# Attention and two FFNs on one core: key sums moved to TensorE, products regrouped over the array's tiles, and new urgencies for the planner

## The chip, the core and the metric

One core of a Trainium2 chip runs the whole program. The metric is device microseconds (us) of one execution; the time of the kernel before is the median of three runs. Beside them one execution was profiled, and all rows below are of that one.

## The reference, cut to what matters

```python
q_lm = q.reshape(B, H, m, S // m, D).mean(axis=3)       # B=4, H=8, S=576, D=64, m=32
k_lm = k.reshape(B, H, m, S // m, D).mean(axis=3)       # sums over 18 neighbours
A, Bm, C = sm(q, k_lm), sm(q_lm, k_lm), sm(q_lm, k)     # sm = softmax(scale * a @ b.T)
Z = Bm.T / (norm_1(Bm) * norm_inf(Bm) + 1e-06)
for _ in range(6):
    Z = 2 * Z - Z @ Bm @ Z                              # inverse of Bm by Newton steps
x = A @ Z @ C @ v                                       # (2304, 512) after the heads are joined
h = x @ w_in;  x = maximum(0.01 * h, h) @ w_out         # first FFN, width 2048
# RMS norm, then silu(x @ w_gate) * (x @ w_val) @ w_out2, width 1536
```

## The kernel before

Nothing loops at run time. A planner in the kernel's own Python code (`Order`) writes out one instruction list for each engine. Each piece of work is a generator that yields its engine, a cost in ns and what it needs (`yield [("pe", 400)], [...]`), and then issues its instructions. Among the pieces that could start soon the planner takes the one with the least due time plus penalties; `PAR` holds the due times and, for each stretch of planned time, a window and a bias for VectorE (DVE), ScalarE (ACT) and GpSimd (POOL). For many pieces two or three engines may be named, and the planner chooses. `"pe"` is a full 128x128 product, `"pet"` a product on a part of the array ("tiled"); `TURN` is what the planner charges for a change between them. The costs decide the order only. On the chip every engine runs its list in that order and waits on semaphores.

The work of the batches of attention is called a chain. That of the first batch (`chain(0)`) stands alone at the start, before there is any other work for TensorE, and so sets when the first FFN can begin:

- `key_sums` and `sums` add 18 neighbouring columns of K and Q. For the first batch, K's are done by a halving add on POOL and a reduction on DVE.
- The scores Q_lm K^T (L653, four groups, each four products at 64x32 tiles) go to DVE for sums and to ACT for copies; then come softmax, norms, the Gram matrix (`gram`, L758), transposes of the exponentials (`turn`, L797), five Newton steps (L925, each followed by an add on DVE) and the sixth, folded into z (L895). C V is L825, its small transposes L864.
- `soft_a` (L976) makes the scores of A, `soft_rest` its softmax on DVE, POOL and ACT. It needs the key sums. For the first batch `times_z` (L1041) multiplies the result by z, and `split_a` writes it as a high and a low part, `at`.
- `form_first` (L1121) multiplies W_in by the small matrix of C V in four column pieces. The result is `mm`, which is split likewise.
- `ffn1_h` (L1168, six products of 128x288) multiplies `mm` and `at`; `ffn1_y` (L1239, twelve products) multiplies by W_out. These two fill TensorE until the gated FFN (L1641) and the output product (L1916). The chains of the batches 1 to 3 are strewn among them.
- Weights arrive in halves of 64-bit words and are turned into float32 by ACT (L496, L504), POOL and DVE (`convert`).
- `warm` issues spare products on a tile of ones (L1072), whose results nobody reads, wherever the planner sees TensorE free before the first FFN.

Each group of four heads takes four tiles of the array: `heads` gives for head h the rows of its operand and a strip `32 * (h ^ g)` of 32 partitions, so that in L1041 row strip and column strip of a product are the same, for both groups.

## Time and profile before

| | us |
|---|---|
| median of three runs | 792.68 (792.26 to 792.8) |
| the profiled execution | 791.7 |
| its span, first to last instruction | 789.6 |
| TensorE busy with products in that span | 777.4 |

The span is what the views count in; the execution's own time holds 2.1 us more around it. In the views PE is TensorE's products, PEld its weight loads. A float32 product leaves two records in the trace (a transpose, and a product of the type float32r, one), so counts there are twice those of the instruction list.

### The profile page before, as it was taken

To read this page: it belongs to the slowest core of one execution; us is meant where nothing else is said; L and a number is where in the kernel's file an instruction comes from. 1 tells how busy PE (TensorE), PEld (TensorE's weight loads), DVE (VectorE), ACT (ScalarE), POOL (GpSimd) and SP (SyncE) were. 2 spreads that over 40 slices of the span, in tenths; PEclk is the share of its full clock that TensorE was granted. 3 is DMA by queue.
4 is the path that set the end of the run, shared out by engine and by line. 5 is a ranking of instruction groups with operands and counts; after the bars stand their busy time and mean duration, and the time that the engine had idled before them with its cause. 6 is when DMAs were issued, how large, how long until landed. Compare 5 with 4: busy or idle time off the path is not lost.

```text
span 789.6 us, 16701 instructions
## 1 busy us (share of the span) xinstructions
PE 777.4 (98%) x6489; PEld 740.6 (94%) x6489; DVE 537.7 (68%) x1044; ACT 391.3 (50%) x862; POOL 219.8 (28%) x262
## 2 busy tenths in 40 slices
PE   5999999999999999999999999999999999999998
PEld 3788998899799998999999999999999999999998
DVE  6899966866631488876588666544357599997771
ACT  4887465555554565656643333234432265454440
POOL 2421000154575200035443533466541010000000
PEclk9999999999999999999999999999999999999999
DMA  9984645484653353544211433222331695535501
GB/s 327 364 288 145 240 137 168 117 285 155 181 171 131 108 194 127 191 126 129 81 41 64 164 114 114 94 68 86 114 115 41 193 330 174 169 115 167 154 28 54
DMA packets 84319, 119.71 MB, mean 152 GB/s; under 512 B 7824, under 2 KB 62608, under 8 KB 84240
## 3 DMA queue, kind: packets, MB, share of 16 engines
q1 hardware_dynamic: 84240, 118.64, 45.7%
q8 instruction: 51, 0.84, 0.4%
q14 instruction: 28, 0.23, 0.1%
HBM read 81.86 MB, written 36.77 MB: 150 GB/s over the span
## 4 chain that ended last, share of the span: by engine, by line
PE 96%; DVE 1%; DMA 1%; ACT 1%; issue 0%; SPq 0%
PE py L1239 25%; PE py L1641 19%; PE b L1641 14%; PE b L1168 13%; PE py L1916 10%; PE b L1916 7%; PE b L1096 2%; DMA kt<-kT 1%; PE b L925 1%; PE b L976 1%; PE b L1072 1%; PE b L797 1%; PE b L825 1%; PE b L653 1%; PE py L653 0%; PE b L1471 0%
## 5 line engine op out<-in xcount | busy, mean ns | idle before, releaser
L1239 PE MATMUL py<-gs,w 128*128 128x288 f32 x1536 | 222.9, 296 | 0.4 <-DVE w L89 0.4
L1239 PEld LDWEIGHTS py<-gs,w 128*128 128x128 f32 x1536 | 209.3, 188 | 5.5 <-issue 3.7
L1168 PE MATMUL b<-at,mm 128*128 128x288 f32 x768 | 119.9, 298 | 0.0
L1168 PEld LDWEIGHTS b<-at,mm 128*128 128x128 f32 x768 | 106.6, 188 | 7.9 <-issue 3.0
L1186 ACT ACTIVATE gs<-b 128x288 fp32r<-128x288 f32 x128 | 52.8, 412 | 105.0 <-PE b L1168 83.3
L89 POOL TENSOR_TENSOR gs<-hs,gs 128x288 fp32r<-128x288 f32 x60 | 53.0, 888 | 115.6 <-ACT hs L1189 86.5
L89 DVE TENSOR_TENSOR ct<-gs,py 128x384 f32<-128x384 f32 x72 | 39.6, 551 | 44.2 <-PE py L1641 42.6
L89 DVE TENSOR_TENSOR gs<-gs,py 128x384 f32<-128x384 f32 x72 | 39.7, 552 | 19.0 <-PE py L1641 17.9
L1189 ACT ACTIVATE hs<-b 128x288 f32<-128x288 f32 x128 | 52.5, 410 | 0.0
L1711 ACT ACTIVATE hs<-b 128x384 f32<-128x384 f32 x36 | 17.7, 491 | 68.8 <-PE b L1641 68.7
L89 POOL TENSOR_TENSOR misc<-misc 128x256 f32<-128x256 f32 (+2 forms) x44 | 34.5, 794 | 31.9 <-DVE misc L89 22.6
L89 DVE TENSOR_TENSOR gs<-hs,b 128x384 f32<-128x384 f32 (+1 forms) x45 | 23.6, 524 | 28.7 <-PE b L1641 24.3
L89 DVE TENSOR_TENSOR gs<-hs,gs 128x288 fp32r<-128x288 f32 x68 | 31.5, 463 | 16.3 <-ACT hs L1189 15.9
L89 POOL TENSOR_TENSOR mm<-misc,mm 128x512 fp32r<-128x512 f32 (+1 forms) x15 | 16.7, 1111 | 85.8 <-ACT mm L450 78.1
L450 ACT COPY hs<-b 128x384 f32<-128x384 f32 (+1 forms) x44 | 19.9, 452 | 36.8 <-PE b L1641 21.5
L1740 ACT ACTIVATE ct<-ct 128x384 f32<-128x384 f32 x36 | 18.9, 526 | 37.5 <-DVE ct L89 37.3
L1641 PE MATMUL b<-w,wt 128*128 128x384 f32 x180 | 35.4, 337 | 0.0
L1641 PE MATMUL b<-w,mm 128*128 128x384 f32 x180 | 35.4, 337 | 0.0
L496 ACT ACTIVATE raw<-raw 128x512 f32<-128x512 f32 x52 | 34.8, 678 | 0.4 <-DMA raw<-w_gate 0.4
L1641 PE MATMUL py<-w,wt 128*128 128x384 f32 x180 | 34.5, 338 | 0.0
L1641 PE MATMUL py<-w,mm 128*128 128x384 f32 x180 | 34.3, 336 | 0.0
L1641 PEld LDWEIGHTS b<-w,wt 128*128 128x128 f32 x180 | 31.9, 188 | 0.0
(306 smaller groups left out, 1594.2 us busy)
## 6 DMA issues: line engine op xcount, KB each, us to landing
u_dram<-us SPq DMA_DIRECT2D x36, 384.0 KB, 2.3
raw<-w_out SPq DMA_DIRECT2D x20, 512.0 KB, 4.4
y_dram<-ys SPq DMA_DIRECT2D x56, 144.0 KB, 2.1
yin<-u_dram SPq DMA_DIRECT2D x20, 384.0 KB, 5.2
raw<-w_gate SPq DMA_DIRECT2D x12, 512.0 KB, 4.0
raw<-w_val SPq DMA_DIRECT2D x12, 512.0 KB, 4.8
wo_dram<-raw SPq DMA_DIRECT2D x42, 128.0 KB, 2.0
qt<-qT SPq DMA_DIRECT2D x8, 576.0 KB, 4.9
```

The source lines that it names most:

```text
L89: self.last = make(*args, **kwargs)
L450: nc.scalar.copy(out, src)
L496: nc.scalar.activation(high.bitcast(F32), high.bitcast(F32), AF.Prelu, scale=2.0 ** -112, alpha=2.0 ** 32)
L1096: nc.tensor.matmul(pm[g][lm, :], wt_in[b, g][rows, p], w_in_sb[c][rows, 2 * g + p, :].bitcast(F32), start=True, stop=True,)
L1168: nc.tensor.matmul(ph[:, :SB], w[b, c][:, g, o:o + P], x[j][:, g, :], start=(n == 0), stop=(n == 3 * NG - 1),)
L1186: nc.scalar.activation(g_hi[u], ph[:, :SB], AF.Prelu, alpha=0.01)
L1189: nc.scalar.activation(hs, ph[:, :SB], AF.Prelu, alpha=0.01)
L1239: nc.tensor.matmul(yacc[i][d][:, :SB], w[f][:, d * P:(d + 1) * P], x[u], start=(f == f0 and n == 0), stop=(f == f1 - 1 and n == 2),)
L1641: nc.tensor.matmul(pp[:, :GB], w[f][:, i, c * P:(c + 1) * P], x[b][k][:, c, :], start=(first and n == 0), stop=(n == 5), skip_group_check= ...
L1711: nc.scalar.activation(sg, pp["a"][:, :GB], AF.Silu)
L1740: nc.scalar.activation(t["c12"], t["c12"], AF.Silu)
L1916: nc.tensor.matmul(pp[name][:, :HM], x[:, p, :], o_home[r][:, i, p, :], start=(tag is not None and m == 0), stop=(m == 3 * NP2 - 1), skip_ ...
```

## The change

Seven edits, all in code of the first batch but for the tables:

1. `key_sums`: instead of an add on POOL and a reduction on DVE, 18 products with the identity for each of the two groups add up the 18 neighbours in PSUM (128x128 weights, 64 columns, float32), in slices of six; ACT or DVE copies the result.
2. `soft_a` of the first batch writes head h to strip 32 h in both groups, `z` is made in the same layout (in two banks, copied out by two copies), and `times_z` multiplies row strip 32 h into column strip `32 * (h ^ g)`: the two groups lie on eight different tiles and no longer on the same four.
3. `warm` may issue a small tiled spare product where the last product was tiled.
4. Pieces of the first batch that were planned as full products are named tiled, with smaller costs: scores, Gram matrix, Newton steps, z, `times_z`, `form_first`.
5. `TURN` between two tiled pieces falls from 80 to 40.
6. All numbers in `PAR` are new.
7. `split_a` and the output step have slightly different planned costs.

```diff
-        [13.0, 1837, 1.2, 2906, -16456, 25637],
+        [13.0, 1517, 19.7, -11610, -23885, -30083],
...
-    TURN = {("pe", "pet"): 89, ("pet", "pet"): 80, ("pet", "pe"): 104}
+    TURN = {("pe", "pet"): 89, ("pet", "pet"): 40, ("pet", "pe"): 104}
...
-            half = et[:, g, :S].rearrange("p (a m t) -> p a m t", a=2, t=GRP // 2)
-            yield pool(S), [f"k0,{g}"]
             x = k_in[0, g][:, :, :S].rearrange("p a (m t) -> p a m t", t=GRP)
-            nc.gpsimd.tensor_add(half, x[..., :GRP // 2], x[..., GRP // 2:])
-            yield dve(S), []
-            nc.vector.reduce_sum(k_in[0, g][:, :, S:], half, axis=AX.X)
+            step = 6
+            for i in range(0, GRP, step):
+                yield [("pe", 112 * step)], [] if i else [("px", 1), f"k0,{g}"]
+                if i == 0:
+                    pk = bank("px")
+                for t in range(i, i + step):
+                    nc.tensor.matmul(
+                        pk[:, :2 * M], ident, x[..., t], start=(t == 0), stop=(t == GRP - 1)
+                    )
+            on = yield act(2 * M) + dve(2 * M), []
+            copy(on, k_in[0, g][:, :, S:], pk[:, :2 * M].rearrange("p (a m) -> p a m", m=M))
+            order.free(pk)
...
-                yield [("pe", 420)], [(pa, 1)]
-                pr = bank(pa)
+                yield [("pet", 330)], [(pa, NG)]
+                pz = [bank(pa) for _ in range(NG)]
...
-                                pr[lm, g * M:(g + 1) * M], rz[lm, 2, g, :], r,
+                                pz[g][M * h:M * h + M, :M], rz[lm, 2, g, :], r,
...
-            for _, p, rows, lm in heads(g):
+            for h4, p, rows, lm in heads(g):
+                if b == 0:
+                    lm = slice(M * h4, M * h4 + M)
...
-        yield [("pe", 1100)], [(tag, NG), ("at_hi", 1), "z", "rs0"] + [
+        yield [("pet", 560)], [(tag, NG), ("at_hi", 1), "z", "rs0"] + [
...
+                own = slice(M * h, M * h + M)
                 nc.tensor.matmul(
-                    ps[g][lm, :SB], zt[lm, g, :], x_in[j, g][lm, :],
+                    ps[g][lm, :SB], zt[own, g, :], x_in[j, g][own, :],
...
-            nc.tensor.matmul(spare[0][:, :SB], fill[:, :P], fill, start=True, stop=True)
-            yield [("pe", PAR["fill"][order.now > 7000])], []
+            if order.form == "pe":
+                nc.tensor.matmul(spare[0][:, :SB], fill[:, :P], fill, start=True, stop=True)
+            else:
+                small = fill[:M, :72].bitcast(F32)
+                nc.tensor.matmul(
+                    spare[0][:M, :72], small[:, :M], small, start=True, stop=True
+                )
+            yield [(order.form, PAR["fill"][order.now > 7000])], []
```

The change moves line numbers: L1072, L758, L797, L925, L976, L1041, L1121, L1168 and L1239 of before are L1082, L765, L804, L931, L984, L1050, L1136, L1183 and L1254 after, and the key sums' products are L677.

**TensorE, from the start to the second Newton step.** Before (`py` and `b_` are banks of PSUM, `gs` the tile of ones, `bb` the softmax of the landmarks, `rz` the Newton matrices, `e` the exponentials):

```order
L1072 MATMUL b_141<-gs 128x288 x6
L653 MATMUL py<-kt,qsum_146 32x288 x8
L653 MATMUL py<-kt,qsum_152 32x288 x8
L976 MATMUL b_198<-qt,kt 32x288 x4
L1072 MATMUL b_141<-gs 128x288
L976 MATMUL b_216<-qt,kt 32x288 x4
L1072 MATMUL b_141<-gs 128x288 x11
L758 MATMUL py<-bb 32x32 x8
L1072 MATMUL b_141<-gs 128x288 x24
L797 MATMUL py<-ident,e 128x128 x6
L925 MATMUL py<-rz 32x2x32 x8
```

After:

```order
L1082 MATMUL b_141<-gs 128x288 x22
L653 MATMUL py<-kt,qsum_151 32x288 x8
L653 MATMUL py<-kt,qsum_163 32x288 x8
L677 MATMUL b_203<-kt,ident 128x64 x12
L677 MATMUL b_226<-kt,ident 128x64 x6
L677 MATMUL b_203<-kt,ident 128x64 x6
L677 MATMUL b_226<-kt,ident 128x64 x6
L765 MATMUL py<-bb 32x32 x8
L677 MATMUL b_226<-kt,ident 128x64 x6
L984 MATMUL b_285<-qt,kt 32x288 x4
L984 MATMUL b_301<-qt,kt 32x288 x4
L804 MATMUL py<-ident,e 128x128 x8
```

Sixteen spare products more stand ahead of the first scores and 27 fewer behind them; the 36 key sums and all eight products of L984 now stand ahead of the transposes and the first Newton step. After the last row come two more transposes and then the first Newton step (L931). Spare products number 43 before and 32 after; none of the 32 is of the small tiled kind.

**ScalarE, from the landmarks' exponentials on.** Before, with what each row waits for in brackets:

```order
L737 ACTIVATE e,sm<-e,mx 128x32
L708 ACTIVATE e,sm<-e,mx 128x576 [waits DVE_49,Activation_49]
L496 ACTIVATE raw<-raw 128x512 [waits DMAHW0_49]
L708 ACTIVATE e,sm<-e,mx 128x576 [waits Activation_49]
L1000 ACTIVATE x_203<-x_203 128x288 [waits Pool_49]
L504 ACTIVATE raw<-raw,half 128x512
```

After:

```order
L744 ACTIVATE e,sm<-e,mx 128x32
L450 COPY kt<-b_203 128x2x32 [waits PE_49]
L715 ACTIVATE e,sm<-e,mx 128x576 [waits DVE_49,Activation_49]
L715 ACTIVATE e,sm<-e,mx 128x576 [waits Activation_49]
L450 COPY kt<-b_226 128x2x32 [waits PE_49]
L496 ACTIVATE raw<-raw 128x512 [waits DMAHW0_49]
L504 ACTIVATE raw<-raw,half 128x512
```

The two copies of the key sums stand between the exponentials, and the first conversion of a weight (L496) stands behind both.

**TensorE at the first FFN's beginning.** Before, from z's successors on:

```order
L1121 MATMUL py<-w_in,wt 32x128 x8
L1041 MATMUL py<-ys,zt 32x288 x8
L1121 MATMUL py<-w_in,wt 32x128 x8
L1121 MATMUL b_555<-w_in,wt 32x128 x4
L1121 MATMUL b_556<-w_in,wt 32x128 x4
L1168 MATMUL b_570<-at,mm 128x288 x6
L1168 MATMUL b_586<-at,mm 128x288 x6
```

After:

```order
L1136 MATMUL py<-w_in,wt 32x128 x8
L984 MATMUL b_546<-qt,kt 32x288 x4
L1050 MATMUL py<-ys,zt 32x288 x8
L1183 MATMUL b_583<-at,mm 128x288 x6
L1183 MATMUL b_596<-at,mm 128x288 x6
L1136 MATMUL b_608<-w_in,wt 32x128 x4
L1136 MATMUL b_609<-w_in,wt 32x128 x4
```

Before, three of the four pieces of `form_first` stand ahead of the first product of the FFN; after, two (the first of them earlier, between Newton steps), and the last two pieces stand among the FFN's products.

Over the whole program TensorE's list changes the form of its tiles 123 times before and 127 times after; behind the first product of the FFN it is 100 and 102 times. Spare products and key sums apart, every line of TensorE has as many products as before. Of the work that several engines may do, 21 of the subtractions behind `ffn1_h` and some others went from DVE to POOL (DVE 1046 instructions before, 991 after; POOL 267 and 296; ACT 848 and 873).

## Rows read from the trace of the kernel before

**Rows 1.** Page: busy us of each engine (share of the span), instructions.

```profile
PE 777.4 (98%) x6489; PEld 740.6 (94%) x6489; DVE 537.7 (68%) x1044; ACT 391.3 (50%) x862; POOL 219.8 (28%) x262
```

**Rows 2.** What TensorE waited for: line, releaser, us in total, times, longest.

```profile
PE py L653 <- DMA kt<-kT: 5.0, 1, 5.0
PE b L976 <- DVE kt L89: 1.7, 2, 1.2
PE b L1072 <- POOL gs L89: 1.4, 1, 1.4
PE py L1121 <- issue: 0.5, 1, 0.5
PE py L1239 <- DVE w L89: 0.4, 1, 0.4
```

**Rows 3.** TensorE in order of time: start, us, instructions, idle before.

```profile
1.35 1.81 PE L1072 MATMUL b<-gs 128*128 128x288 f32 x6 [1.35 <-POOL gs L89]
8.12 3.57 PE L653 MATMUL py<-kt,qsum 64*32 64x288 f32 x32 [4.96 <-DMA kt<-kT]
...
16.95 3.43 PE L1072 MATMUL b<-gs 128*128 128x288 f32 x24
20.21 0.82 PE L797 MATMUL py<-ident,e 128*128 128x128 f32 x6
20.96 0.42 PE L925 MATMUL py<-rz 32*32 32x64 f32 x16
...
21.90 0.43 PE L925 MATMUL py<-rz 32*32 32x64 f32 x16
22.26 0.69 PE L976 MATMUL b<-qt,kt 64*32 64x288 f32 x8
22.88 0.43 PE L925 MATMUL py<-rz 32*32 32x64 f32 x16
23.23 1.73 PE L825 MATMUL py<-vt,et 128*32 128x64 f32 x80
...
28.89 1.17 PE L1041 MATMUL py<-ys,zt 32*32 32x288 f32 x16
29.99 0.45 PE L1121 MATMUL py<-w_in,wt 64*32 64x128 f32 x16
30.23 0.42 PE L1121 MATMUL b<-w_in,wt 64*32 64x128 f32 x16
30.59 2.81 PE L1168 MATMUL b<-at,mm 128*128 128x288 f32 x18
```

**Rows 4.** TensorE's weight loads by form, 0 to 60 us: busy us, mean ns.

```profile
L1239 PEld LDWEIGHTS py<-gs,w 128*128 128x128 f32 x108 | 14.7, 188 | 2.6 <-issue 1.0 <-DVE w L89 0.6 <-ACT rawe L496 0.5
L925 PEld LDWEIGHTS py<-rz 32*32 32x32 f32 x80 | 1.3, 104 | 1.5 <-ACT w L450 0.6 <-DVE rz L89 0.5 <-issue 0.4
L864 PEld LDWEIGHTS py<-ident,t 32*64 32x64 f32 x16 | 0.4, 129 | 0.2
```

**Rows 5.** The scores' queue waits (count: ns min/median/max, first to last start).

```profile
L653 PEldq EVENT_SEMAPHORE  x2: 51/51/51, 8.0 to 9.4; - x2
```

**Rows 6.** VectorE in order of time.

```profile
11.74 0.46 DVE L89 TENSOR_REDUCE e<-py 128x16 f32<-128x288 f32 x1 [0.50 <-PE py L653]
12.11 0.74 DVE L89 TENSOR_REDUCE kt<-et 128x64 f32<-128x576 f32 x1
...
19.30 0.40 DVE L89 SCALAR_TENSOR_TENSOR rz<-py,al,ident 128x32 f32<-128x32 f32 x2
```

**Rows 7.** ScalarE in order of time.

```profile
16.11 0.66 ACT L496 ACTIVATE raw<-raw 128x512 f32<-128x512 f32 x1
...
29.85 0.92 ACT L1054 ACTIVATE at<-py,trs 128x288 fp32r<-128x288 f32 x2
```

**Rows 8.** Busy us of each engine in two stretches: PE, PEld, DVE, ACT, POOL, PEclk.

```profile
30.00:35.00 5.00, 5.00 (x80) 4.38 (x76) 4.90 (x14) 5.00 (x17) 2.17 (x3) 1.00 1.02 399
40.00:50.00 10.00, 9.64 (x88) 8.37 (x80) 9.98 (x19) 8.97 (x21) 2.45 (x4) 1.00 0.59 195
```

More of the change, by code (lines that the diff above doesn't have):

```diff
@@ L40 @@
-        [585.3, 1406, 791.2, 11248, -56391, -3858],
-        [907.5, 613, 110719.1, 26830, -13262, -86],
-        [9999, 186, 828.9, -24040, 2929, -7317],
-    ],
-    "hold": 25,
-    "t0": 6194,
-    "unit": 2763,
-    "chain": [33891937, 27814, 77403, 128623],
-    "soft": 6565,
-    "form": 3499,
-    "conv": 726,
-    "load": 18091,
-    "raw": -738,
-    "v": [9885693, 36195, 0, -663],
-    "q": -983,
-    "h": 55,
-    "y": -4185,
-    "norm": 144565,
-    "last": 43604,
-    "second": 179503,
@@ new lines @@
+        [9999, 45440, 5916.6, -4252, 7383, 71345],
+    ],
+    "hold": 195,
+    "t0": -97038,
+    "unit": 2719,
+    "chain": [4750371, 28638, 81295, 110688],
+    "soft": 5812,
+    "form": 3339,
+    "conv": 0,
+    "load": -531,
+    "raw": -8611,
+    "v": [2321835, 94264, 54378, 10375],
+    "q": -1435,
+    "h": -8,
+    "y": -4014,
+    "norm": 247198,
+    "last": 55962,
+    "second": 4457,
+    "unit2": 1564,
+    "pair": 27310358,
+    "o_from": 1052356,
+    "o_step": 19635,
+    "load_u": [14412, -100020, -5798167930],
@@ L77 @@
+    "prep_u": 507,
+    "prep": 2319,
+    "form0": -984,
+    "soft_h": 5489866,
+    "fill": [215, 140],
+    "soft1": 294,
+    "timesz": 11224554,
+    "alone": 1447,
+    "with": 305156,
+    "spread": [4661, -4680418, -84073, -128300],
+    "load_o": 18041,
+    "split_o": -131007,
 }
@@ L895, in chain @@
                             nc.tensor.matmul(
-                                pr[lm, g * M:(g + 1) * M], rz[lm, 2, g, :], r,
+                                pz[g][M * h:M * h + M, :M], rz[lm, 2, g, :], r,
                                 start=(i == 0), stop=(i == 1), skip_group_check=True,
                             )
-                yield dve(NG * M), []
-                nc.vector.tensor_copy(
-                    zt, pr[:, :NG * M].rearrange("p (g m) -> p g m", m=M)
-                )
-                order.free(pr)
+                for g in range(NG):
+                    yield dve(M), []
+                    nc.vector.tensor_copy(zt[:, g, :], pz[g][:, :M])
+                order.free(*pz)
                 order.done("z")
@@ L908, in chain @@
                 return
-            needs, ns = [(pt, 1)], 168 if b else 350
+            needs, ns = [(pt, 1)], 168
             if b == 0:
@@ L919, in chain @@
             order.task[0] += PAR["spread"][b]
-            yield [("pet" if b else "pe", ns)], needs
+            yield [("pet", ns)], needs
             pr = bank(pa)
@@ L970, in soft_a @@
         before += [f"{x}{b},{g}" for g in gs for x in ("ksum", "q")]
-        yield pet(SB) if j > 1 else pe4(SB), [("pt", len(gs)), ("x2", len(gs))] + before
+        yield pet(SB) if j > 1 else [("pet", 530)], [("pt", len(gs)), ("x2", len(gs))] + before
         ps = [bank("px") for _ in gs]
@@ L1110, in form_first @@
         for k in range(NP):
-            yield [("pe", 400)], [("py" if k < 2 else "px", NG), f"w_in0,{k}"] + before
+            yield [("pet", 260)], [("py" if k < 2 else "px", NG), f"w_in0,{k}"] + before
             if k == 0:
@@ L1906, in step @@
         def step(name, l, r, tag=None, needs=()):
-            yield pe(HM, 3 * NP2, -20), list(needs) + ([(tag, 1)] if tag else []) + [
+            yield pe(HM, 3 * NP2, -12), list(needs) + ([(tag, 1)] if tag else []) + [
                 f"U{n},{l}", f"wo{r}"
```

45 lines of the change are left out of this document (15 added, 30 removed).

## The prediction

> **What bounds the kernel now.** I read the page first: TensorE holds products for 777.4 us of a span of 789.6 [rows 1], so 12.2 us are left, and no edit that frees another engine can give more than TensorE's queue lets through. The view of waits says where they lie: five lines, 9.0 us together, and all but 0.4 of that (L1239) stands in the first batch's prologue [rows 2]. Then I read TensorE in order of time. The first scores wait for a key until 8.12, the first Newton step starts at 20.96, the first product of the FFN at 30.59 [rows 3]. From there TensorE hardly stops, so the end is the start of that product plus the work behind it. The change can act in three ways: it moves 30.59, it adds or removes TensorE work behind it, or it makes TensorE wait there. Lastly I read VectorE, ScalarE and the weight loads in the prologue, to see which of them the Newton chain follows.
>
> **Spare products ahead of the scores.** In the profile four groups of scores take 3.57 us, 0.89 each; the same form later takes 0.62 (22.26 to 22.88) [rows 3]. I read the first as TensorE's lower level of 1.2 GHz after 4.96 us without work, the second as 2.4 GHz. Now 22 spare products precede them. At 0.30 each (1.81 us for six) or 0.14 each (3.26 us for 24) they end between 4.4 and 8.0, so TensorE is idle for 0.1 to 3.7 us ahead of the scores, not 4.96. I expect the higher level at 8.12. Two groups then end at 9.4. The third cannot start before the second key is there, at 9.4 to 9.5 [rows 5]. So the scores end at 10.7 instead of 11.7: a gain of 1.0. The bounds are 0 and 1.0.
>
> **Key sums on TensorE.** DVE loses two reductions of 0.74 [rows 6] and POOL two adds; TensorE gets 36 float32 products, 72 records, each with its own load of 128 columns. No row shows this form. The lower bound is the stream alone: a spare product of 288 columns costs 0.136, so 64 columns cost 0.030, twice for each record, 72 x 0.060 = 4.3 us. The upper bound is the spacing of spare products, which carry such a load: 72 x 0.136 = 9.8 us. Between them I ask whether the load or the stream is longer. Loads of 32, 64 and 128 columns show as 104, 129 and 188 ns [rows 4], so 96 columns more cost 84 ns, and 128 columns occupy the load path for some 0.11 us, while the stream of a record needs only 0.06. The nearest row agrees: six transposes, each with a load of its own of 128 columns, take 0.75 us to the next work [rows 3]; less some 0.1 for the change of tiles behind them that is 0.108 each. (The 0.1 is an estimate: four passes of 0.136 are 0.54 of the 0.62 of a group of L976.) I take 72 x 0.108 = 7.8 us, so the kernel's own planned cost of 36 x 0.112 = 4.0 is too low by half.
>
> The Trainium skill bears on this: the page "TensorE: Matmul & The Clock Gate", section "LDWEIGHTS (loading the stationary operand)", gives a load's time as its columns divided by 1.2 GHz, whatever the rows. By that an estimate for 72 loads of 128 columns is 7.7 us; a planner that counts streams alone would have 4.0. The trace's slope of 84 ns for 96 columns speaks for the page and against the plan.
>
> **Up to the first Newton step.** In the new order this step stands behind all of it: scores to 10.7, a change of tiles and the key sums to 18.6, the Gram product inside them (0.3 with its changes) to 18.9, eight products of L984 to 20.1, ten transposes at 0.108 to 21.2, a change, 21.3. Both groups of L984 now lie on the same four tiles, which I count as twice 0.62 less one change. Before, it was 20.96, behind 24 spare products and six transposes [rows 3]. So the step comes 0.3 later, though nothing but its place in the queue holds it: on DVE the last reduction of the scores began at 11.74 and the matrices at 19.30 [rows 6], 7.6 us; even without the work that leaves DVE they would be ready at 18.7.
>
> **From there to the first FFN product,** 9.63 us before. Both lists hold five Newton steps, spaced 0.94 and 0.98 where nothing stands between (20.96, 21.90, 22.88), and L825 with 1.73. What differs: `times_z` on eight tiles takes about 0.65 instead of 1.10 (28.89 to 29.99), -0.45; one of the pieces of `form_first` (two take 0.60 from 29.99 to 30.59) moves behind the FFN's first products, -0.3; four products of L984 now stand between z and `times_z`, +0.6; ten spare products instead of one, up to 9 x 0.14 = 1.3 where they are in the way, nothing where the step waits for DVE anyway; I take +0.3. The separate copies of z cost DVE one small instruction, +0.1. The sum is +0.2, with bounds -0.2 and +1.2. `split_a` begins 0.74 ahead of the first FFN product (29.85 to 30.59) [rows 3, 7], and I leave that. The first FFN product then starts at 31.1, 0.5 later.
>
> **Behind it.** One piece of `form_first` more: +0.3. Two changes of tiles more (102 for 100): +0.2. The second `times_z`: -0.45. The wait of 0.4 at L1239 [rows 2] may go as conversions keep their lead or not; I take -0.2. Sum -0.15, bounds -0.6 and +0.5. The subtractions that went from DVE to POOL take longer there, but TensorE has a product of L1239 and one of L1168 of work between; cover gone, each late one costs at most what it is late. The products of both FFNs are the same in number and form, and I count 0.
>
> The Trainium skill, page "TensorEngine Tiling (Array Packing)", section "Key Properties", says that a change of tiling mode drains TensorE. By this the four changes more of the whole list (127 for 123) are the price of grouping, an estimate of 0.4 us at the row's 0.1, which the terms above hold already.
>
> **Sum.** +0.3 +0.2 -0.15 = +0.35 on the profiled execution's 791.7; the median lies 1.0 above that, at 792.68. I predict 793.0, no change that can be told: about 0.2%, 1.6 us, is what a measurement of this kernel can tell from none (791.1 to 794.3).
>
> **The rivals.**
> - *The loads hide behind the streams* and the key sums take 4.3 us. For it speaks that loads and products overlap everywhere else (740.6 us of loads in the same span [rows 1]); against it that everywhere else the streams are longer. The first Newton step comes at 17.8, 3.2 earlier. DVE's bound of 18.7 is then no bound, since its reductions and softmax pieces have left that stretch. Of the 3.2 I expect some 0.8 back, because ScalarE and VectorE are full when the FFN starts (5.00 and 4.90 of 5 us; VectorE 9.98 of 10 later [rows 8]) and must convert W_out for L1239. Time 792.7 - 3.2 + 0.2 - 0.15 + 0.8 = 790.4. Chance 0.27.
> - *ScalarE is blocked* (the other side). Its copy of the second key sum stands ahead of its first conversion of a weight, which ran at 16.11 [rows 7] and now cannot before the key sums end at 18.9 and the copy is done at 19.2: 3.1 later. With ScalarE and VectorE full from 30 on [rows 8], this is made up only in the prologue. If less than half of it is, the first pieces of `form_first` and the first products of L1239 wait for W_in and W_out: up to 3.1 less the 0.5 by which TensorE is late itself, some 2.3 us. Time 795.2. It decides from 1.6 us of waits on. Chance 0.13.
> - *The clock falls back* between the spare products and the scores, as it did before over 4.96 us. The scores take 0.89 a group again (+1.0) and the first key sums run at 1.2 GHz too (+0.5). Time 794.5. Against it speaks that the idle time is at most 3.7. Chance 0.10.
> - *A part does nothing*: none of the 32 spare products is of the new small form, so the edit of `warm` shows only in the number and the places. That changes no term above.
>
> **How the numbers follow.** My forecast has 0.50 (own range 792.1 to 794.4), the rivals 0.27, 0.13 and 0.10. The range takes in the first and most of the second: 790.0 to 795.0. Faster by over 0.2%: nearly all of the first rival and a twentieth of the rest, 0.28. Slower: the second rival, half of the third and a little of my own, 0.20. Within: 0.52.
>
> **What would show it.** L677's records 0.108 apart (7.8 us in all) or 0.06 (4.3); the scores at 0.62 a group or 0.89; the first Newton step (L931) at 21.3 and the first L1183 at 31.1; L1050 at 0.65; waits of TensorE behind 31 us at most 0.6 in sum. I am wrong if the first L1183 comes before 29, if waits behind it exceed 1.6 us, or if the work behind it is longer or shorter than 759 us by more than 1.

## The result, and the profile after

The changed kernel takes 797.44 us (median of five runs, 796.49 to 799.04); the kernel before took 792.68 beside it. The ratio is 1.0058, with a 95% interval from 1.0042 to 1.0074: slower by some 4.6 us, where 793.0 was predicted and 790.0 to 795.0 given as the range. The profiled execution took 797.52 us with a span of 795.7, 6.1 more than before.

The page of the changed kernel, busy time of each engine with its share of the span and its instructions, beside [rows 1]:

```profile
PE 785.1 (99%) x6550; PEld 747.9 (94%) x6550; DVE 523.0 (66%) x989; ACT 404.6 (51%) x887; POOL 245.7 (31%) x291
```

TensorE holds products for 7.7 us more (the key sums alone for 9.1); VectorE has 14.7 less, GpSimd 25.9 more. What TensorE waited for, beside [rows 2] (line, releaser, us in total, times, longest):

```profile
PE py L653 <- DMA kt<-kT: 2.4, 2, 2.1
PE b L1082 <- POOL gs L89: 1.4, 1, 1.4
PE b L1183 <- DVE us L89: 1.1, 1, 1.1
PE b L1050 <- DVE ys L89: 0.8, 1, 0.8
PE b L1183 <- ACT at L1063: 0.6, 1, 0.6
PE py L1656 <- DVE gs L89: 0.4, 1, 0.4
PE py L1254 <- POOL gs L89: 0.4, 1, 0.4
```

The prologue's waits fell from 8.6 to 3.8, as the change meant. But where one wait of 0.4 stood behind the start of the FFN, there are now four of 2.7 in sum and one of 0.6 right ahead of it. TensorE in order of time, beside [rows 3] (start, us, instructions, idle before):

```profile
7.96 1.18 PE L653 MATMUL py<-kt,qsum 64*32 64x288 f32 x16 [2.12 <-DMA kt<-kT]
9.39 1.18 PE L653 MATMUL py<-kt,qsum 64*32 64x288 f32 x16 [0.25 <-DMA kt<-kT]
10.50 7.44 PE L677 MATMUL b<-kt,ident 128*128 128x64 f32 x60
17.87 0.33 PE L765 MATMUL py<-bb 32*32 32x32 f32 x16
18.13 1.68 PE L677 MATMUL b<-kt,ident 128*128 128x64 f32 x12
19.74 1.17 PE L984 MATMUL b<-qt,kt 64*32 64x288 f32 x16
...
22.08 0.43 PE L931 MATMUL py<-rz 32*32 32x64 f32 x16
...
30.69 0.71 PE L1050 MATMUL py<-ys,zt 32*32 32x288 f32 x16
32.02 2.17 PE L1183 MATMUL b<-at,mm 128*128 128x288 f32 x12 [0.62 <-ACT at L1063]
```

The scores take 0.59 a group. Sixty key-sum records take 7.37 us to the next work (17.87 less 10.50), 0.123 each. The first Newton step comes at 22.08 (before 20.96), the first product of the FFN at 32.02 (before 30.59), 1.43 late. From there to the end it is 763.7 us, where it was 759.1: **4.6 of the 6.1 us lie behind the prologue**, where I had counted -0.15.

Two stretches show where. First 300 to 360 us, the view by stretches, columns as in [rows 8], first the kernel before, then the changed one:

```profile
300.00:360.00 60.00, 60.00 (x463) 59.00 (x461) 48.85 (x89) 34.05 (x87) 11.15 (x11) 1.00 0.49 159
```

```profile
300.00:360.00 60.00, 58.75 (x449) 57.29 (x448) 31.30 (x46) 35.02 (x87) 40.81 (x42) 1.00 0.46 147
```

GpSimd's work there has grown from 11 operations to 42, and TensorE now stands for 1.25 us. The cause stands in the changed kernel's VectorE (first two rows), GpSimd (the next two) and TensorE (the last two):

```profile
339.50 0.46 DVE L89 SCALAR_TENSOR_TENSOR misc<-b,misc 128x288 f32<-128x288 f32 x1 [5.42 <-ACT misc L1496]
340.90 9.27 DVE L89 SCALAR_TENSOR_TENSOR b<-misc 128x288 f32<-128x288 f32 x1 [0.94 <-ACT misc L1502]
...
340.28 1.87 POOL L89 TENSOR_TENSOR q<-yin,q 128x768 fp32r<-128x768 f32 x1
...
348.00 1.84 POOL L89 TENSOR_TENSOR q<-misc,q 128x768 fp32r<-128x768 f32 x1
...
349.17 1.75 PE L1254 MATMUL py<-gs,w 128*128 128x288 f32 x12
352.05 1.05 PE L1183 MATMUL b<-at,mm 128*128 128x288 f32 x6 [1.13 <-DVE us L89]
```

An operation of 288 columns, of a kind that takes 0.46 in the row above it, stands for 9.27 us, from 340.90 to 350.17. In this time GpSimd runs seven operations back to back (four of 768 columns, three of 288 between them), and VectorE ends 0.33 after the last (349.84). Everything behind it on VectorE is late, and TensorE with it. In the kernel before, subtractions of 768 columns for the same tile (`q`) stand on VectorE:

```profile
338.73 0.95 DVE L89 TENSOR_TENSOR q<-yin,q 128x768 fp32r<-128x768 f32 x1
```

### The profile page after: what moved, and what is told of

The parts are those of the page before. It is cut to its first block, busy times and chain, and to the rows that moved or that the text cites. A ratio compares the mean times of both kernels' runs of the same rounds, so it can differ in the third digit from the quotient of the medians.

```text
span 795.7 us, 16823 instructions
## 1 busy us (share of the span) xinstructions
PE 785.1 (99%) x6550; PEld 747.9 (94%) x6550; DVE 523.0 (66%) x989; ACT 404.6 (51%) x887; POOL 245.7 (31%) x291
## 4 chain that ended last, share of the span: by engine, by line
PE 92%; DVE 4%; DMA 2%; ACT 1%; issue 1%; POOL 0%; SPq 0%; DVEq 0%
PE py L1254 24%; PE py L1656 17%; PE b L1656 13%; PE b L1183 12%; PE py L1931 10%; PE b L1931 7%; PE b L1111 2%; DMA kt<-kT 2%; DVE b L89 1%; PE b L677 1%; PE b L931 1%; PE b L984 1%; PE b L804 1%; PE b L832 1%; PE b L653 1%
## 5 line engine op out<-in xcount | busy, mean ns | idle before, releaser
L1254 PE MATMUL py<-gs,w 128*128 128x288 f32 x1536 | 222.5, 296 | 0.4 <-POOL gs L89 0.4
L1254 PEld LDWEIGHTS py<-gs,w 128*128 128x128 f32 x1536 | 209.0, 188 | 6.8 <-issue 5.3
L1183 PE MATMUL b<-at,mm 128*128 128x288 f32 x768 | 119.5, 297 | 1.8 <-DVE us L89 1.1
L1183 PEld LDWEIGHTS b<-at,mm 128*128 128x128 f32 x768 | 106.5, 188 | 8.7 <-issue 2.5
L89 POOL TENSOR_TENSOR gs<-hs,gs 128x288 fp32r<-128x288 f32 x81 | 67.1, 832 | 68.7 <-ACT hs L1204 54.2
L89 POOL TENSOR_TENSOR misc<-misc 128x256 f32<-128x256 f32 (+2 forms) x47 | 40.5, 866 | 66.1 <-DVE us L89 40.5
L1755 ACT ACTIVATE ct<-ct 128x384 f32<-128x384 f32 x36 | 18.9, 524 | 39.2 <-DVE ct L89 39.1
L496 ACT ACTIVATE raw<-raw 128x512 f32<-128x512 f32 x52 | 35.3, 679 | 3.6 <-DMA raw<-w_val 3.5
L450 ACT CAST mm<-misc 128x512 fp32r<-128x512 f32 (+2 forms) x36 | 23.3, 658 | 26.5 <-POOL misc L89 14.6
L1656 PE MATMUL b<-w,wt 128*128 128x384 f32 x180 | 35.4, 337 | 0.0
L1656 PE MATMUL b<-w,mm 128*128 128x384 f32 x180 | 35.4, 337 | 0.0
L1656 PE MATMUL py<-w,wt 128*128 128x384 f32 x180 | 34.9, 339 | 0.2
L1656 PE MATMUL py<-w,mm 128*128 128x384 f32 x180 | 34.4, 336 | 0.4 <-DVE gs L89 0.4
L1656 PEld LDWEIGHTS py<-w,wt 128*128 128x128 f32 x180 | 31.6, 188 | 0.8 <-DVE gs L89 0.8
L1656 PEld LDWEIGHTS py<-w,mm 128*128 128x128 f32 x180 | 31.6, 188 | 0.7 <-DVE gs L89 0.7
L1656 PEld LDWEIGHTS b<-w,wt 128*128 128x128 f32 x180 | 31.9, 188 | 0.0
```

What stands on the lines that cost most here:

```text
L89: self.last = make(*args, **kwargs)
L450: nc.scalar.copy(out, src)
L496: nc.scalar.activation(high.bitcast(F32), high.bitcast(F32), AF.Prelu, scale=2.0 ** -112, alpha=2.0 ** 32)
L1183: nc.tensor.matmul(ph[:, :SB], w[b, c][:, g, o:o + P], x[j][:, g, :], start=(n == 0), stop=(n == 3 * NG - 1),)
L1254: nc.tensor.matmul(yacc[i][d][:, :SB], w[f][:, d * P:(d + 1) * P], x[u], start=(f == f0 and n == 0), stop=(f == f1 - 1 and n == 2),)
L1656: nc.tensor.matmul(pp[:, :GB], w[f][:, i, c * P:(c + 1) * P], x[b][k][:, c, :], start=(first and n == 0), stop=(n == 5), skip_group_check= ...
```

## The experiments

The reasons to be told apart: **A**, TensorE's queue ahead of the first Newton step, lengthened by the key sums, sets the end; **B**, ScalarE and VectorE, full from 30 us on, set it; **C**, GpSimd's new work stops VectorE behind 300 us. This table gives the profiled execution's first Newton step, first product of the FFN and the time from that to the end of the span, and the ratio of the medians to the kernel before with its interval. Medians of the kernel before lie between 792.4 and 793.4 in the five series, so the ratios are what compares.

| kernel | Newton | FFN | behind it | ratio |
|---|---|---|---|---|
| before | 20.96 | 30.59 | 759.1 | 1 |
| changed | 22.08 | 32.02 | 763.7 | 1.0058 (1.0042 to 1.0074) |
| e1 four blocks | 29.32 | 39.27 | 764.2 | 1.0140 (1.0126 to 1.0155) |
| e2 two blocks | 21.77 | 31.91 | 764.3 | 1.0052 (1.0037 to 1.0066) |
| e3 two of 18 | 17.64 | 28.54 | 763.1 | 1.0011 (1.0002 to 1.0019) |
| e4 four subtractions | 21.79 | 31.73 | 762.1 | 1.0031 (1.0019 to 1.0043) |
| e5 six spares | 22.59 | 32.54 | 762.9 | 1.0063 (1.0051 to 1.0075) |
| e6 copies on VectorE | 22.04 | 31.99 | 762.5 | 1.0058 (1.0045 to 1.0072) |
| e7 key sums off TensorE | 21.32 | 31.41 | 762.6 | 1.0037 (1.0025 to 1.0049) |
| e8 three edits | 18.86 | 33.77 | 761.2 | 1.0056 (1.0043 to 1.0069) |
| e9 before, spares | 20.12 | 31.49 | 759.0 | 0.9987 (0.9977 to 0.9997) |
| e10 before, eight tiles | 22.67 | 32.35 | 758.8 | 1.0001 (0.9988 to 1.0013) |
| e11 before, both | 18.79 | 30.66 | 760.1 | 0.9986 (0.9973 to 0.9998) |
| e12 before, new urgencies | 19.31 | 29.52 | 766.4 | 1.0059 (1.0042 to 1.0075) |
| e13 changed, old urgencies | 33.75 | 44.58 | 766.0 | 1.0257 (1.0241 to 1.0273) |
| e14 before, 10 long spares | 19.63 | 29.93 | 758.4 | 0.9995 (0.9981 to 1.0009) |
| e15 seven subtractions | 23.35 | 33.30 | 761.4 | 1.0023 (1.0013 to 1.0034) |
| e16 before, 18 long spares | 18.73 | 29.77 | 758.7 | 0.9977 (0.9965 to 0.9990) |

### What the key sums cost: e1, e2, e3

```diff
 e1 (e2 the same with blocks of 64)
+for s in (slice(c, c + M) for c in range(0, P, M)):
     nc.tensor.matmul(
-        pk[:, :2 * M], ident, x[..., t], start=(t == 0), stop=(t == GRP - 1)
+        pk[s, :2 * M], ident[s, s], x[s][..., t], ...
 e3
+if t in (0, GRP - 1):
     nc.tensor.matmul(pk[:, :2 * M], ident, x[..., t], ...)
```

> The changed kernel with one edit, every instruction in the same place: each key-sum product with the 128x128 identity becomes four products with its 32x32 blocks on the diagonal, so a load has 32 columns and not 128, but there are 288 records for 72. In the profile of after the 72 records start 0.120 us apart (8.7 us), and small tiled records elsewhere 0.020 to 0.028 apart (C V: 64 records in 1.3). So the key sums should take 6 to 8 us. Theory A (TensorE's queue ahead of the first Newton step sets the end): the first Newton step comes earlier by what the key sums save, 0.7 to 2.7 us, from 22.08 to 19.4 to 21.4, and the whole time falls by the same, 797.4 to between 794.7 and 796.7. Theory B (ScalarE and VectorE set the end from 30 us on): the first Newton step comes earlier, but waits behind 30 us grow by the same and the time stays at 797.4, within 0.5. Theory C (a wait at 350 us made by GpSimd and VectorE): the wait of 1.1 at 350 us stays under either.

> As the run with four blocks, but with two 64x64 blocks on the diagonal: 144 records. If a record costs what its load's columns cost (129 ns for 64 columns against 188 for 128 where the rows show durations), they lie some 0.06 apart and the sum is again near 8.7 us and the first Newton step near 22; if two tiles load side by side, 0.03 apart and 4.3 us, the first Newton step at about 18.5 to 19.5, held by VectorE's matrices. Theory A: the time follows the first Newton step one for one, 794 to 797.4. Theory B: 797.4 within 0.5 either way.

> The changed kernel with 2 of the 18 products of each group of key sums; the other 16 are left out, so the key sums hold 2 of their 18 terms. All else stands in its place. It takes 7.7 us of products out of the stretch ahead of the first Newton step, so this step is held by VectorE alone, at some 18 to 19 us instead of 22.08. Theory A: the time falls by the 3 to 4 us by which the step is earlier, to some 794. Theory B: the first product of the FFN comes earlier, but waits behind 30 us take it back, and the time stays above 796. Theory C: the wait of 1.1 at 350 stays in both.

e2's key sums on TensorE, then e3's step and first product of the FFN:

```profile
10.29 7.39 PE L678 MATMUL b<-kt,ident 64*64 64x64 f32 x120
```

```profile
13.48 0.33 PE L766 MATMUL py<-bb 32*32 32x32 f32 x16 [2.36 <-DVE bb L89]
...
17.64 0.65 PE L932 MATMUL py<-rz 32*32 32x64 f32 x16
...
28.54 2.18 PE L1184 MATMUL b<-at,mm 128*128 128x288 f32 x12 [0.63 <-ACT at L1064]
```

Half the columns per load cost half the time per record (0.061 for 0.123), and the sum is the same: neither a fixed cost per record nor the stream, which has 64 columns in both, sets the 0.123, but the load. Why two tiles side by side bring nothing e2 does not say: the prediction's 0.060 for a record's stream would account for 0.061 as well. e3 leaves out most of the key sums (its sums hold 2 of 18 terms); the FFN begins 3.5 earlier, the work behind it is 763.1, and the span falls by 4.1. So A holds for the prologue, one for one, and B does not. But e3, whose FFN begins 2.05 before that of the kernel before, is still not faster than it. e1 was a miss of another kind: its many small products were not slow (0.030 apart, four for one of the 0.123), but TensorE stood twice with nothing to wait for, 1.71 and 2.47 us, and its granted clock was 0.50 from 18.9 to 22.3 us and at 26 to 28:

```profile
11.85 5.24 PE L678 MATMUL b<-kt,ident 32*32 32x64 f32 x168
18.79 2.33 PE L678 MATMUL b<-kt,ident 32*32 32x64 f32 x72 [1.71 <-issue]
...
24.99 0.42 PE L678 MATMUL b<-kt,ident 32*32 32x64 f32 x8 [2.47 <-issue]
```

### GpSimd against VectorE: e4, e15

```diff
 e4: split_steps of the gated FFN's first block
     e = yield pool(n) + dvep(n), []
+    if on_dve:
+        e = "dve"
     engine[e].tensor_sub(lo, src, hi.bitcast(F32))
 e15: also y1_sub
+    if e == "pool":
+        e = "dve"
```

> The changed kernel with one edit, every other instruction in its place: the four subtractions of 768 columns for the gated FFN's first block, which GpSimd does at 339 to 348 us, are issued on VectorE. Theory C (while GpSimd works without a pause, an operation of VectorE stood for 9.27 us where it takes 0.45 elsewhere, and TensorE waits 1.13 for it): the long operation goes, the wait at 350 goes, and the time falls by 1.1 to 1.8, to 795.6 to 796.3. Its rival (VectorE is late by its own load; four more operations of about 0.9 make it later): the wait at 350 stays or grows and the time is 797.4 or more. The prologue is the same in both: first Newton step at 22.1, first product of the FFN at 32.0.

> The changed kernel with the four subtractions of 339 to 348 us on VectorE, as before, and three more that GpSimd does at 300 to 410 us (768 columns, and 192 and 576 columns at 406.9 and 408.3, where three operations of VectorE take 2.83 us that take 1.35 alone); every other instruction in its place. Theory (contention there too): VectorE gains 1.5 us by its three and loses 1.1 by the two more, so TensorE's loss of 1.15 between 407 and 431 shrinks by about 0.4 and the time lies 0.4 under that of the first run of this kind (ratio 1.0031 to before), at 1.0021 to 1.0030. Rival (VectorE is just full there): the loss stays or grows, ratio 1.0031 or more.

VectorE and TensorE in e4, at the same places:

```profile
340.60 0.45 DVE L89 SCALAR_TENSOR_TENSOR b<-misc 128x288 f32<-128x288 f32 x1
```

```profile
348.69 1.75 PE L1254 MATMUL py<-gs,w 128*128 128x288 f32 x12
350.29 0.94 PE L1183 MATMUL b<-at,mm 128*128 128x288 f32 x6
```

The operation takes 0.45 again, though VectorE now has the four subtractions as well, and the wait is gone: from that L1254 to the next L1183 it is 1.60, where the changed kernel had 2.88 (349.17 to 352.05). C holds, and its rival (VectorE late by its own load) falls. Of the 1.6 by which the work behind the FFN's start is shorter than the changed kernel's (762.1 for 763.7), 0.8 is not this edit's: the changed kernel's profiled execution has the wait of 0.8 at L1050, which e5, e6 and e7, with the same work there, have not; they take 762.5 to 762.9. The medians say 0.27%, with intervals that just meet. e15 moves three more. Of VectorE, the changed kernel, then e15:

```profile
407.32 2.83 DVE L89 TENSOR_TENSOR ys<-ys,misc 128x288 f32<-128x288 f32 x3
```

```profile
407.13 1.18 DVE L89 TENSOR_TENSOR ys<-ys,misc 128x288 f32<-128x288 f32 x3
...
409.17 0.35 DVE L89 TENSOR_TENSOR misc<-q,yin 128x192 f32<-128x192 f32 x1
409.44 0.75 DVE L89 TENSOR_TENSOR misc<-ys,yin 128x576 f32<-128x576 f32 x1
```

The three give back 1.65 and the two more cost 1.10; TensorE's products from 410.49 to 420.11 in the changed kernel take 8.73 us here (410.30 to 419.03) and not 9.62. The ratio came to 1.0023, in the expected band; its interval still touches e4's 1.0031. Together these seven moved operations are about 0.35% of the 0.58%, by the difference of two medians' ratios.

The Trainium skill, page "SBUF — State Buffer", section "SBUF: two separate sides", says that an operation of VectorE with two inputs in SBUF and one of GpSimd that reads SBUF exclude each other, and that the one that starts first has the port for its whole instruction. Trace and e4 agree that they exclude each other. By the page's words I would expect VectorE to have its turn when the operation of GpSimd that ran at 340.90 ended, at 342.15; it got none until the seventh had ended.

### The clock and ScalarE's copies: e5, e6

```diff
 e5: warm
+    n_spare[0] += 1
+    if 6 < n_spare[0] <= 22:
+        pass
 e6: key_sums
-    copy(on, k_in[0, g][:, :, S:], pk[...])
+    copy("dve", k_in[0, g][:, :, S:], pk[...])
```

> The changed kernel with 6 in place of 22 spare products ahead of the first scores, all else in its place. Theory (spare products hold the clock up): TensorE stands idle for some 4.8 us ahead of the scores, not 2.1, the granted clock falls, the four groups of scores take 0.89 each and not 0.59, the first key sums run at the lower level too, and the first Newton step comes 1.0 to 1.8 later, at 23.1 to 23.9; the time is 798.4 to 799.2. Rival (the spare products do nothing): scores at 0.59 a group, the time 797.4.

> The changed kernel with the two copies of the key sums issued on VectorE in place of ScalarE, all else in its place, so that ScalarE's exponentials and its first conversion of a weight no longer stand behind the key sums; that conversion should run at some 15 us in place of 19.95. Theory B (ScalarE is blocked by those copies and cannot make it up): of the waits behind 30 us (0.62 for ScalarE's part of at, 0.35 for gs, 0.78 for ys) at least 1 us goes and the time falls to 795.7 to 796.5. Rival (the lead of the conversions is enough either way, since the run with 2 of 18 key sums gave all 4.1 us back and kept the 0.62 and the 0.35): the waits stay and the time is 797.4 within 0.5. The first Newton step stays at 22.1 in both, since TensorE's queue holds it.

e5's TensorE, then e6's ScalarE:

```profile
7.53 3.55 PE L653 MATMUL py<-kt,qsum 64*32 64x288 f32 x32 [4.36 <-DMA kt<-kT]
11.01 7.44 PE L677 MATMUL b<-kt,ident 128*128 128x64 f32 x60
...
22.59 0.43 PE L931 MATMUL py<-rz 32*32 32x64 f32 x16
```

```profile
14.79 0.66 ACT L496 ACTIVATE raw<-raw 128x512 f32<-128x512 f32 x1
```

With six spares the scores take 0.89 a group, and from key to Newton step it is 15.06 where it was 14.12. So the spare products do what they are for, 0.94 us; but the key sums were at full speed already. The ratio (1.0063 for 1.0058) can't tell: 0.94 us is 0.12%, as much as half an interval. In e6 the first conversion of a weight runs 5.16 earlier than in the changed kernel (19.95), the waits of 0.6 and 1.1 at L1183 and of 0.4 at L1254 and L1656 are all still there, and the ratio is the same: the rival B falls a second time. In e4 to e8 the wait of 0.8 at L1050 is absent or has another place; VectorE, ahead of it, waits 1.52 us at 38 us for a load of K, which lands sooner or later from one execution to the next.

### Taking the key sums back: e7, e8

```diff
 e7: key_sums, in the places of the products and of the copy
+nc.gpsimd.tensor_add(half, x[..., :GRP // 2], x[..., GRP // 2:])
+nc.vector.reduce_sum(k_in[0, g][:, :, S:], half, axis=AX.X)
 e8: e7 and e4, and five spare products in each of the first five places
+nc.tensor.matmul(pk[:, :SB], g_all[:, :P], g_all[:, :SB], start=True, stop=True)
```

> The changed kernel with the key sums as before the change (an add on GpSimd, a reduction on VectorE, 0.74 each there), all other instructions in their places; the sums are complete. If the key sums on TensorE are the prologue's whole loss, the time comes to that of the run with 2 of 18 (794.1) or a little over, since VectorE's two reductions stand in its chain: first Newton step at 17.6 to 19.2, time 794.1 to 795.6. If the sums on VectorE and GpSimd were what held the chain before, the first Newton step stays near 21 and the time above 796. In the first case TensorE stands idle for some 3 to 4 us between the scores and the Gram product, and the clock falls there as in the run with 2 of 18.

> Three edits on the changed kernel, the other instructions in their places: key sums as before the change (GpSimd and VectorE), 25 spare products in the places of the first 30 key-sum products, and the four subtractions at 339 to 348 us on VectorE. If what was found adds up: the spare products keep the clock at its higher level, the first Newton step comes at 17 to 18.5 in place of 22.08, the first product of the FFN at 27.5 to 29 in place of 32.02, the wait at 350 is gone, and the time is 797.4 - 4.1 - 1.8 = 791.5, from 790.8 to 792.8, which is below the kernel before (793.06 with all its runs). If waits behind 30 us take part of it back (the rival, ScalarE and VectorE full), it is 793.5 or more.

Both missed. In e7 the Gram product waits 3.78 us for VectorE's softmax (2.36 in e3), with a reduction of 0.74 in the midst of it, and the granted clock is 0.50 from 16 to 22 us. e8 left the reductions there and filled the wait with spare products: the Gram product waits 0.29, the first Newton step comes at 18.86, and then:

```profile
20.15 1.37 PE L834 MATMUL py<-vt,et 128*32 128x64 f32 x63
23.63 0.57 PE L834 MATMUL py<-vt,et 128*32 128x64 f32 x17 [2.11 <-issue]
```

TensorE stood for 2.11 us in the middle of a row of equal products, waiting for nothing that the profile shows, and worked at the lower level (granted clock 0.50) from 24.1 until 30.9 us. So the gain of 3.2 was lost before the FFN began, at 33.77 and not at 32.02.

### Single parts on the kernel before: e9, e10, e11

```diff
 e9: warm (16 spare products from behind the Gram product to the front)
+    for _ in range(17 if n_spare[0] == 6 else 0 if 24 < n_spare[0] <= 40 else 1):
         nc.tensor.matmul(spare[0][:, :SB], fill[:, :P], fill, start=True, stop=True)
 e10: z, soft_a and times_z of the change, with the old planned costs
+    own = slice(M * h, M * h + M)
-    ps[g][lm, :SB], zt[lm, g, :], x_in[j, g][lm, :],
+    ps[g][lm, :SB], zt[own, g, :], x_in[j, g][own, :],
 e11: e9 and e10
```

> The kernel before with one part of the change alone: 16 of its spare products move from behind the Gram product (24 there) to the front (22 ahead of the scores, 8 left behind), every other instruction of every engine in its place. Theory (the spare products hold the clock, and this part is worth what was predicted): the scores run at 0.59 a group and end some 1 us earlier, VectorE's matrices and the first Newton step follow, from 20.96 to some 19.9, the first product of the FFN from 30.59 to 29.6, and the time is 792.5 - 1.0 = 791.5, from 791.0 to 792.0. Rival (the run with 6 spares lost 0.9 in the prologue and nothing at the end): waits behind 30 us take it, the time stays within 0.4 of before.

> The kernel before with another part alone: the probabilities of the first batch times the inverse on eight tiles (z in two banks, two copies on VectorE for one), every other instruction in its place. In the profiles the step took 1.10 us before and 0.71 after, to the next work. Theory: both of its steps (the first stands right ahead of the FFN, the second among its products) save 0.4, less 0.2 for the second copy; the time falls by 0.2 to 0.8. Rival: ScalarE's and VectorE's split of the result decides what comes next and the time stays within 0.2.

> The kernel before with both of these parts, the spare products moved to the front and the step on eight tiles, every other instruction in its place; key sums, urgencies and planned costs as before. If the two gains add, the first product of the FFN comes at 29.2 in place of 30.59 and the time is 792.5 - 1.2 to - 1.9 = 790.6 to 791.3, faster than both kernels. If the work behind 30 us is held by ScalarE, VectorE or GpSimd, it is 792 to 793.

In e9 the scores stayed at 0.89 a group, the Newton step came 0.84 earlier than before, and the first product of the FFN, behind a wait of 1.93 in `form_first`, 0.90 later. In e11 the Newton step came 2.17 earlier, and the first product of the FFN 0.07 later:

```profile
18.79 0.42 PE L924 MATMUL py<-rz 32*32 32x64 f32 x16
...
25.37 0.41 PE L1125 MATMUL py<-w_in,wt 64*32 64x128 f32 x4
27.89 0.67 PE L1125 MATMUL py<-w_in,wt 64*32 64x128 f32 x12 [2.11 <-issue]
...
30.66 4.16 PE L1172 MATMUL b<-at,mm 128*128 128x288 f32 x18
```

Again a wait for nothing that the profile shows, and then products at the lower level (granted clock 0.50 from 28 to 34 us; 18 in 4.16, where [rows 3] have 2.81). Neither theory of mine had this. The eight tiles alone (e10) shorten their step (0.71 for 1.17) and are worth nothing that the ratio can show: its interval is some 2 us wide.

### The two halves of the change: e12, e13

e12 is the kernel before with the changed `PAR`, e13 the changed kernel with the old `PAR`; nothing else differs, but the planner writes new lists.

```diff
 e12 (all numbers of PAR; e13 the other way round)
-        [13.0, 1837, 1.2, 2906, -16456, 25637],
+        [13.0, 1517, 19.7, -11610, -23885, -30083],
```

> The kernel before with the new numbers of PAR alone (no other edit; the planner writes new lists). Theory (the loss behind 30 us, 4.6 us between before and after, comes from the places that the new urgencies give to work on VectorE and GpSimd, and not from the edits of the code): the work from the first product of the FFN to the end is 762 us or more where the kernel before has 759.1, with waits of 0.3 to 1.4 for VectorE or GpSimd at 300 to 430 us, and the time is 794.5 or more. Rival (the new urgencies are sound and the edits of the code cost the time): 759 to 760 behind the first product of the FFN, a time of 793.5 or less.

> The changed kernel's code (key sums on TensorE, eight tiles, new planned costs, TURN of 40) with the numbers of PAR of before; the planner writes new lists. Theory (the urgencies make the loss behind 30 us, the key sums one in the prologue): the first product of the FFN comes some 1 to 3 us later than before (30.59), since 36 key-sum products of 0.120 a record stand in TensorE's queue, the work behind it is 759 to 761, and the time is 793.5 to 796. Rival (a plan made with other numbers than those it was tuned with is worse wherever it comes from): 763 or more behind the first product of the FFN and a time of 797 or more.

e12, without a line of the new code, gives the ratio of the whole change (1.0059 for 1.0058): the FFN begins 1.07 earlier than before, and 7.3 us are lost behind it. That spoke for the urgencies as the cause. But it is in the main another loss. The operation that stood for 9.27 us takes 1.11 in e12, and TensorE does not stand from 300 to 360 us, though GpSimd has 35.24 us of work there:

```profile
341.56 1.11 DVE L89 SCALAR_TENSOR_TENSOR b<-misc 128x288 f32<-128x288 f32 x1
```

```profile
300.00:360.00 60.00, 60.00 (x462) 59.00 (x461) 34.69 (x63) 40.31 (x97) 35.24 (x36) 1.00 0.57 184
```

Its longest waits behind the FFN's start are 1.3 at L1916 and 1.1 at L1096, which the changed kernel has not; only the 0.4 at L1641 (L1656 there) is common to both. That the ratios are equal is chance. And e13 says otherwise: with the old urgencies the new code has 766.0 behind the FFN's start (which comes 14 us late there), as bad as e12, and both together 763.7. So the rival held for the part behind 30 us: either half alone is worse than both. That urgencies belong to the code they were sought with is argued from these two. e13's prologue was a miss as well, and tells something of the key sums:

```profile
7.58 2.15 PE L653 MATMUL py<-kt,qsum 64*32 64x288 f32 x16 [4.42 <-DMA kt<-kT]
...
14.48 13.06 PE L677 MATMUL b<-kt,ident 128*128 128x64 f32 x60
27.47 1.19 PE L984 MATMUL b<-qt,kt 64*32 64x288 f32 x8
```

With 6 spares ahead and key sums between the scores, a record costs 0.217 (12.99 for 60): by these times TensorE works at its lower level from 9.65 to 27.47 us, without a pause. (The view's granted clock, 1.00 there, has no entry before 33.9 us.)

### The wait that the profile can't name: e14, e16

```diff
 warm, on e11 (fill and the bank taken over 512 columns); e16 has 15 for 7
+    for _ in range(7 if n_spare[0] == 6 else n_spare[0] % 2 if n_spare[0] <= 26 else 0):
         nc.tensor.matmul(spare[0], fill[:, :P], fill, start=True, stop=True)
```

> The kernel before with the step on eight tiles and spare products of 512 columns in place of 288, half as many: 10 ahead of the scores, 10 behind them, 20 in all for 43; every other instruction in its place. TensorE's list is 23 products shorter up to the FFN. Theory (the supply of instructions): TensorE again stands after its 345th product, which is now in the middle of the step on eight tiles and no longer in form_first, until about 1.5 us behind the second transfer of instructions; the wait is shorter than the 2.11 of the run with 43, some 0.7 to 1.5, and the time is 790.8 to 791.8. Rival (the wait belongs to the place, form_first, and its weights): the wait stays where it was, in form_first after its first four records, and the time is that of the run with both parts, 792.1.

> As the run with long spare products, but 18 of 512 columns ahead of the scores in place of 10, so that TensorE works until about 7.3 us and stands 0.2 to 1.1 us until the key is there. Theory (the clock held the run with 10 back): scores at 0.59 a group, the first Newton step at 18.2 to 18.8 and not 19.63, the time 790.5 to 791.3 and less spread over its runs. Rival (the supply of instructions behind the 345th product sets when the FFN begins, whatever stands before it): the Newton steps come earlier, the wait behind the 345th product grows from 1.06 to about 2, and the time is 792.1 as in the other runs with moved spare products.

In e14 the wait went from `form_first` to the middle of the step on eight tiles and fell from 2.11 to 1.06, as expected if the supply of instructions makes it; the time did not follow (792.06 where 790.8 to 791.8 was expected):

```profile
26.90 0.76 PE L1043 MATMUL py<-ys,zt 32*32 32x288 f32 x11
28.73 0.68 PE L1043 MATMUL py<-ys,zt 32*32 32x288 f32 x5 [1.06 <-issue]
```

Counted from the start of the trace, this is behind the 345th product record, as in the kernel before (the 0.5 of L1121 in [rows 2]), e3 (0.47), e9 (1.93), e10 (0.76), e11 (2.11) and e16 (1.57), whatever product that is. The queue of instruction transfers shows one such transfer just ahead of its end, in e9 as follows (packets, MB, share):

```profile
q1 hardware_dynamic: 139, 0.32, 79.2%
q8 instruction: 1, 0.02, 5.3%
```

That is 26.9 to 28 us; this transfer of 16 KB ran from 26.97 to 27.91, and TensorE went on at 29.42. In the nine kernels with such a wait it ends 1.2 to 1.6 us behind a transfer. Only e8's other wait, 1.24 ahead of its second half of L986, has no transfer ahead of it; it ends 0.1 behind VectorE's second reduction of K, as the 0.6 in that place in e7. In e16 the four groups of scores took 2.05 us in all and the Newton step came at 18.73; the wait was 1.57, between the two expectations, and the ratio 0.9977. At a median of 791.29 beside 793.43 **e16 is faster than both kernels**, than the kernel before by 0.1 to 0.35%.

## Why the prediction was wrong

- **Scores at 2.4 GHz, end 10.7: right here, but not to be relied on.** They ended by 10.50. With the same 22 spare products and 2.02 to 2.18 us without work behind them, the profiled runs of e1, e7, e9 and e15 show 0.89 a group, the changed kernel, with 2.12, 0.59, as the other seven with 0.6 to 1.4. So the prediction was right here in part by luck: the rival "the clock falls back" came in four of twelve profiled runs with 22 such products, where I gave it 0.10. It was too dear at 1.5: e5 shows 0.94.
- **Key sums, 72 x 0.108 = 7.8: the mechanism right, the size too small.** They take 0.123 a record, 8.9; the load sets it, as e2 shows (0.061 with half the columns). From this the first Newton step at 22.08 in place of 21.3; scores, L984 and transposes came as summed up. By the rule of the Trainium skill, page "TensorE: Matmul & The Clock Gate", section "LDWEIGHTS (loading the stationary operand)", a load of 128 columns is an estimate of 0.107: near this row, and half of the 0.217 that e13 shows at the lower level. The rival that the loads hide is out.
- **From there to the FFN, +0.2: right in the sum.** 9.94 for 9.63, with L1050 at 0.71; but it holds a wait of 0.62 for `at` that the sum had not, so other terms were less than counted, which is luck. The first product at 32.02 for 31.1 is the key sums' error and little else.
- **Behind it, -0.15: this step failed,** by 4.8 us. It rested on the words that TensorE's products are the same in number and form, and that the subtractions moved to GpSimd "take longer there" under cover: "I count 0". What they cost is not that they take longer but that VectorE stands still beside them. e4 and e15 give back 1.3 of the trace at 350 us and 0.9 at 411 to 420, and 0.35% of the time. The seven operations that they move are not of the 21 behind `ffn1_h` that I had counted, but of the "some others", which I had not looked at. The bound I had named (waits over 1.6, or the work behind by more than 1) was passed: 2.7 and 4.6. Of these, 0.8 is the wait at L1050, which comes and goes with a load of K.
- **The second `times_z`, -0.45:** no run can show it; it is 0.06%, and e10's interval is 0.25% wide.
- **The rival on ScalarE** gave the nearest time, 795.2, for the wrong reason: its first conversion did come 3.8 later (19.95 for 16.11 [rows 7]), but e6 takes that away and the ratio stays.

What e15 leaves open is 2.3 us behind the FFN's start (761.4 for 759.1), part of which is the further piece of `form_first` (0.38, predicted 0.3). Some 0.9 more are waits of 0.2 to 0.4 (1.3 in sum, for 0.4 before) ahead of five different products; the last 1.0 was not isolated, so for that part the cause stays open. A kernel that has the changed lists with e15's moves and cheap key sums was not made, since in e7 and e8 the key sums, put back in their places, brought new waits.

## What to carry to other kernels

A count of equal products says nothing about the work behind the stage one looks at: when a planner's numbers change, compare the busy time of every engine by stretch, and look closely where GpSimd's share has tripled. The share alone proves nothing: e12 has it too, and TensorE loses nothing there. Read VectorE's longest durations against the median of their form; an operation of twenty times its length is a stall, though the profile books it as busy. And before gaining microseconds in a prologue of many small products, see whether TensorE waits there for nothing that the profile names: such a wait kept its place in the count of products here, and in e9, e11 and e16 most or all of what was gained ahead of it was gone again at the FFN's start.

## What the runs showed of the hardware

- An operation of VectorE with both inputs in SBUF stood for 9.27 us through seven operations of GpSimd (changed kernel); with four of them moved away it took 0.45 (e4).
- In the prologue of nine kernels TensorE stands behind the same numbers of product records (218 in e8, e14 and e16; 345 in the kernel before and six others; 222 and 350 in e1) for 0.2 to 2.5 us, until 1.2 to 1.6 us after a transfer of 16 KB of instructions. In eight of the nine other transfers take 72 to 103% of the DMA engines' time meanwhile, in e3 (0.47) some 8%. That the transfer causes the wait is argued from these places and times; no run delayed a transfer alone.
- Records of 64 columns, each with a load of 128 columns, lie 0.123 us apart at TensorE's upper level (changed kernel) and 0.217 at its lower (e13); with a load of 64 columns 0.061 (e2).
